# Summing, scaling and splitting the next chunk's x at set units of the first MoE's work

## The chip, the cores and the metric

The kernel runs on one core of one Trainium2 chip. The core has TensorE (matmuls, in profiles PE, its weight loads PEld), VectorE (DVE), ScalarE (ACT), GpSimd (POOL) and SyncE (SP), which here only issues DMAs. Each takes its own queue in order; they wait for one another by semaphores. The metric is the device time of one execution in microseconds (us); the median of several runs counts.

## The reference

Attention with a block mask over 4 batches x 8 heads (576 tokens of 64), then a gated MLP over all 2304 tokens ("moe1"), then a top-2 MoE with 8 experts. Cut to what matters:

```python
scores = np.where(mask, q @ k.T / 8, -1e9)               # per head, mask of 64x64 blocks
attn = np.exp(scores - scores.max(-1))
x = attn / (attn.sum(-1) + 1e-9) @ v                     # 2304 x 512, heads side by side
h = (x @ w1) * (x @ w2) @ w3                             # moe1
x = h @ w_out
logits = x @ w_gate + log1p(exp(x @ w_noise)) * noise    # router, top 2 of 8 experts
for e in range(8):                                       # moe2
    out[mask_e] += weight * (relu(x[mask_e] @ m1[e]) @ m2[e])
```

All matmuls run in fp32r with operands split into a high part and the rest (three matmuls for one product, `mm3`, L462 to L464).

## The kernel before

Attention goes head by head (32 heads). For each head `prep_h` splits q and k (hi on ScalarE and VectorE, L580 to L583; kl on GpSimd, L585), `s_unit` computes scores (L612, L615), `s_max` their maxima (nm, VectorE L626) and exponentials (pb, ScalarE L631), `g_unit` transposes (tp, L645) and splits the result (pt, ScalarE L649, VectorE L651), `av_a`/`av_b` multiply by v (L658, L670). The unnormalised output of a head goes to DRAM in two halves (x2, L674 on SP); after the last head of a batch the reciprocal sums go there too (rs, L685).

moe1 works on 9 chunks of 256 tokens. For chunk c, `x_load` (L147) reads both halves of x2 into xab (L160) and the reciprocal sums, spread over partitions, into xr (L165), all by SP. `x_prep` (L178) has three steps: the sum of the halves on GpSimd (L183), the scaling on VectorE (L186), and the split into xh (ScalarE L453, VectorE L457). The tiles xab, xr and xh have one buffer each, so the loads of a chunk wait until the scaling and the split of the one before have read their tiles. Then come eight units `ab` (L192): 24 matmuls on xh and the weights pc, a copy on ScalarE (at, L203), a product on VectorE (L204), and a split into gt (ScalarE L453, GpSimd L457). I write unit 3.4 for f = 4 of chunk 3. After the eight units `yout` (L208) multiplies gt by w3 @ w_out, in four blocks, and a `router` of small VectorE steps runs beside the next chunk. During the first units the weights are still converted from 64-bit words (stg, stf, L520 to L522 on VectorE) and split (pc).

`steps` (L361) is a generator that writes all this down; the attention loop draws from it ("f" in the table `LATER`), so heads and moe1 are interleaved, and what is left when the heads end is drawn alone. `ahead(c + 1, step)` writes the next chunk's load and its three preparation steps among the units of chunk c. Chunks 2, 4 and 6 need a batch whose heads end while the chunk before runs; theirs are written when `self.ready` allows. The order in each engine's queue is not the written one: a scheduler sorts the instructions by priority and by its own estimate of time, and `ab` and `yout` are written at a lower priority (`MOE_PRIO`) than the rest, `x_prep` among it.

Of the kernel before, what the change touches and what calls it, by code (L numbers as in the profile page):

```python
# [14 lines left out]
OP = mybir.AluOpType  # L15
# [14 lines left out]
CH = 256  # L30
NCH = NT // CH
# [31 lines left out]
ZC, NF = 3, 10  # L63
PIECE_PRIO, W_PRIO, MOE_PRIO = -60, -400, -200

FIRST = "g0 g1 t f1.3 c t o g2 g3 t p s0 t t s1 s2 f1.3 c t a f1.3 t b0 t s3 h t t c c b1 v l"
# [7 lines left out]
def r32(ap):  # L76
    return ap.bitcast(F32)


class Moe1:  # L80


    def __init__(self, k, p2, psM):
        self.k, self.tc, self.nc, self.a, self.p2 = k, k.tc, k.nc, k.a, p2
        self.psM = self.psR = psM
        self.p2s = ExitStack()
        self.ready, self.rt, self.ticks, self.conv = 0, iter(()), 1, 0
        self.xs, self.gts, self.ys, self.lg = {}, {}, {}, {}
        self.scat = []

    def setup_load(self):
        nc, a, p2 = self.nc, self.a, self.p2
# [99 lines left out]
    def ab(self, c, f):  # L192
        nc, p2, x = self.nc, self.p2, self.xs[c]
        ps = self.psM.tile([P, 512], F32, name="m")
        fo = (f % 2) * P
        for i, n in enumerate(("w1", "w2")):
            w = self.wp[n, f // 2]
            for dt in range(4):
                o = dt * 256 + fo
                self.k.mm3(ps[:, i * CH:(i + 1) * CH], (w[:, 0, o:o + P], w[:, 1, o:o + P]),  # L200
                           (x.h[:, 0, dt, :], x.h[:, 1, dt, :]), dt == 0, dt == 3)
        at = self.p2b.tile([P, CH], F32, name="at", bufs=2)
        nc.scalar.copy(at, ps[:, 0:CH])  # L203
        nc.vector.tensor_tensor(at, at, ps[:, CH:], op=OP.mult)  # L204
        gt = self.gts[c, f] = self.p2b.tile([P, 2, CH], F32R, name="gt", bufs=8)
        self.k.split((gt[:, 0, :], gt[:, 1, :]), at, low="pool")

    def yout(self, c, t, part):  # L208
        nc, p2 = self.nc, self.p2
# [150 lines left out]

    def steps(self):  # L361

        state = {}

        def ahead(c, step):

            if c == NCH or state.get(c, 0) != step or (step == 0 and self.batches(c) > self.ready):
                return
            if step == 0:
                self.x_load(c)  # L370
            else:
                self.x_prep(c, step - 1)
            state[c] = step + 1

        for c in range(NCH):
            for step in range(4):
                while state.get(c, 0) == step:
                    ahead(c, step)
                    yield 0
            for f in range(8):  # L380
                while self.conv < 28 + 4 * (f // 2):
                    yield 0
                with self.tc.high_priority(offset=MOE_PRIO):
                    self.ab(c, f)
                self.tick(self.ticks)
                if c == NCH - 1 and f % 2 == 1:
                    self.k.load_next()
                    self.k.load_next()
                if f in (0, 1, 2):
                    ahead(c + 1, 0)  # L390
                elif f == 4:
                    ahead(c + 1, 1)
                elif f == 6:
                    ahead(c + 1, 2)
                yield 2.67
            ahead(c + 1, 3)
            if c == NCH - 1:
                for _ in self.rt:
                    pass
                self.freeze()  # L400
            for t in range(TPC):
                for part in range(2):
                    with self.tc.high_priority(offset=MOE_PRIO):
                        self.yout(c, t, part)
                    self.tick(self.ticks)
                    yield 2.6
            for _ in self.rt:
                pass
            self.rt = self.router(c)
# [33 lines left out]
class Kernel:  # L443
# [5 lines left out]
    def split(self, dst, src, act="act", low="dve"):  # L449
        nc = self.nc  # L450
        h, l = dst
        if act == "act":
            nc.scalar.copy(h, src)  # L453
        else:
            nc.vector.tensor_copy(h, src)
        eng = nc.vector if low == "dve" else nc.gpsimd
        eng.tensor_tensor(l, src, r32(h), op=OP.subtract)  # L457

    def mm3(self, out, lh, rh, first, last):
        nc = self.nc  # L460
# [576 lines left out]
```

## Time and profile before

| | |
|---|---|
| three runs | 1132.89, 1132.94, 1134.70 us (median 1132.94) |
| the profiled execution | 1133.57 us, of which the span of the core is 1131.8 us |
| mean granted TensorE clock | 0.97 of full speed |
| TensorE busy | 1064.8 us, 94% of the span |
| VectorE, ScalarE, GpSimd busy | 576.9, 495.2, 371.4 us |
| attention and moe1 together | about 140 to 510 us |
| moe1 alone, then moe2 | about 510 to 640 us, then to the end |

A timeline row gives the start, the time it took, the engine, the line and the tiles; in brackets how long the engine had been idle and what ended that. A window row gives busy time in a stretch for each engine, then TensorE's granted clock (1.00 is 2.4 GHz, 0.50 is 1.2 GHz), then DMA. The chain of waits follows the end of the program back to what it hung on. Idle time matters where the engine is the one that the others have to wait for.

### The profile page before, as it was taken

The page shows a single profiled execution, that of the slowest core. Times are in us where ns is not written, and L with a number is a line of the kernel's source. Part 1 is how long each engine was busy: PE and PEld are TensorE (multiplying, and loading weights), DVE is VectorE, ACT ScalarE, POOL GpSimd, SP SyncE. Part 2 cuts the span into 40 slices and gives each one's busy share as a digit, 9 for nine tenths or more (in the row PEclk, how much of TensorE's full clock was granted, in tenths as well). Part 3 has the DMA queues.
Part 4 walks back from the last instruction along what each step waited for, and adds up shares of the span by engine and source line. Part 5 has one row for each costly group of instructions (what it writes and reads, how often), then busy time and mean ns, then how long its engine had stood idle before and what let it go on. Part 6 is the DMA issues. An engine that isn't in the chain of part 4 may idle for free.

```text
span 1131.8 us, 17580 instructions
## 1 busy us (share of the span) xinstructions
PE 1064.8 (94%) x6588; PEld 950.7 (84%) x6588; DVE 576.9 (51%) x1229; ACT 495.2 (44%) x1180; POOL 371.4 (33%) x355
## 2 busy tenths in 40 slices
PE   5899978999899989999999998999999999999996
PEld 3677767899798979998898797989899998989894
DVE  5897779667475847644443533543334342424110
ACT  5765546565466646642233314433333333333120
POOL 4443455525232442414422316332222222120202
PEclk9899988999899999999999999999999999999998
DMA  9765775325432484416213318745454545341203
GB/s 230 235 190 174 186 182 182 98 90 146 135 104 74 147 180 122 88 41 142 42 38 59 121 26 254 208 122 121 122 121 122 121 117 127 102 113 30 38 10 40
DMA packets 79443, 135.82 MB, mean 120 GB/s; under 512 B 21005, under 2 KB 45813, under 8 KB 79349
## 3 DMA queue, kind: packets, MB, share of 16 engines
q1 hardware_dynamic: 69237, 113.44, 35.4%
q0 software_dynamic: 10112, 21.16, 10.0%
q8 instruction: 54, 0.88, 0.3%
q14 instruction: 40, 0.33, 0.1%
HBM read 103.92 MB, written 30.66 MB: 119 GB/s over the span
## 4 chain that ended last, share of the span: by engine, by line
PE 72%; DMA 11%; DVE 10%; issue 3%; ACT 2%; POOL 2%; SPq 1%; POOLq 0%; DVEq 0%; ACTq 0%
PE ph L462 12%; PE ph L464 12%; PE ph L463 12%; PE m L462 7%; PE m L464 7%; PE m L463 7%; PE tp L645 3%; PE av L670 3%; DMA xr<-rs 2%; PE sb L615 2%; PE sb L612 2%; DMA stg<-in_w_dram 2%; PE m L885 2%; DVE stf L521 1%; DVE hi L582 1%
## 5 line engine op out<-in xcount | busy, mean ns | idle before, releaser
L462 PE MATMUL m<-xh,pc 128*128 128x256 f32 x576 | 166.4, 293 | 4.4 <-DVE at L204 2.0
L463 PE MATMUL m<-xh,pc 128*128 128x256 f32 x576 | 163.8, 288 | 2.6 <-DVE xh L457 2.6
L464 PE MATMUL m<-xh,pc 128*128 128x256 f32 x576 | 162.0, 287 | 4.0 <-POOL pc L457 4.0
L462 PE MATMUL ph<-xt,pc 128*128 128x256 f32 (+1 forms) x512 | 157.0, 308 | 4.6 <-ACT xt L453 4.6
L463 PE MATMUL ph<-xt,pc 128*128 128x256 f32 (+1 forms) x512 | 157.4, 308 | 0.0
L464 PE MATMUL ph<-xt,pc 128*128 128x256 f32 (+1 forms) x512 | 157.1, 307 | 0.0
L898 DVE SCALAR_TENSOR_TENSOR ht<-ph,ht 128x256 fp32r<-128x256 f32 (+1 forms) x128 | 61.8, 489 | 131.5 <-ACT ht L897 128.4
L912 POOL DMA_INDIRECT out_dram<-yo,ids x40 | 64.7, 1617 | 195.4 <-ACT yo L911 102.6
L462 PE MATMUL ph<-pc,ht 128*128 128x512 f32 x320 | 128.0, 401 | 0.0
L463 PE MATMUL ph<-pc,ht 128*128 128x512 f32 x320 | 126.3, 395 | 0.0
L464 PE MATMUL ph<-pc,ht 128*128 128x512 f32 x320 | 126.2, 395 | 0.0
L631 ACT ACTIVATE pb<-sb,nm 128x288 f32<-128x288 f32 (+3 forms) x192 | 93.6, 497 | 73.8 <-DVE nm L629 38.8
L457 DVE TENSOR_TENSOR pc<-stf,pc 128x1024 fp32r<-128x1024 f32 x56 | 67.4, 1225 | 102.2 <-ACT pc L453 98.7
L453 ACT CAST pc<-stf 128x1024 fp32r<-128x1024 f32 (+1 forms) x96 | 82.1, 872 | 81.2 <-DMA stf<-in_m_dram 47.9
L462 PEld LDWEIGHTS m<-xh,pc 128*128 128x128 f32 x576 | 110.6, 193 | 6.9 <-DVE at L204 2.9
L464 PEld LDWEIGHTS m<-xh,pc 128*128 128x128 f32 x576 | 110.0, 194 | 4.7 <-POOL pc L457 4.4
L463 PEld LDWEIGHTS m<-xh,pc 128*128 128x128 f32 x576 | 110.5, 193 | 4.0 <-DVE xh L457 3.3
L897 ACT ACTIVATE ht<-ph 128x256 fp32r<-128x256 f32 (+1 forms) x128 | 55.2, 437 | 130.9 <-PE ph L464 129.2
L457 POOL TENSOR_TENSOR gt<-at,gt 128x256 fp32r<-128x256 f32 x72 | 60.4, 841 | 140.2 <-ACT gt L453 137.7
L462 PEld LDWEIGHTS ph<-xt,pc 128*128 128x128 f32 x512 | 96.6, 189 | 5.2 <-ACT xt L453 4.9
L463 PEld LDWEIGHTS ph<-xt,pc 128*128 128x128 f32 x512 | 96.6, 189 | 0.3
L464 PEld LDWEIGHTS ph<-xt,pc 128*128 128x128 f32 x512 | 96.6, 189 | 0.0
(157 smaller groups left out, 2298.8 us busy)
## 6 DMA issues: line engine op xcount, KB each, us to landing
stf<-in_m_dram SPq DMA_DIRECT2D x56, 512.0 KB
qk<-in_qk_dram SPq DMA_DIRECT2D x32, 576.0 KB
stg<-in_w_dram SPq DMA_DIRECT2D x32, 512.0 KB
x<-ev SPq DMA_DIRECT2D x32, 288.0 KB
xab<-x SPq DMA_DIRECT2D x20, 256.0 KB
yt<-y SPq DMA_DIRECT2D x18, 260.0 KB
stg<-in_w_out_dram SPq DMA_DIRECT2D x8, 512.0 KB
v<-in_v_dram SPq DMA_DIRECT2D x24, 160.0 KB
```

The source lines that it names most:

```text
L453: nc.scalar.copy(h, src)
L457: eng.tensor_tensor(l, src, r32(h), op=OP.subtract)
L462: nc.tensor.matmul(out, a, c, start=first, stop=False)
L463: nc.tensor.matmul(out, a, d, start=False, stop=False)
L464: nc.tensor.matmul(out, b, c, start=False, stop=last)
L612: nc.tensor.matmul(o, lh, c.hi[:, 1, k0:k0 + w], start=True, stop=False)
L631: nc.scalar.activation(pb[t][:, k0:k0 + src.free_size()], src, AF.Exp, bias=nm, scale=1.0, accum_out=sums[:, h // H, t + n, h % H:h % H + 1])
L645: nc.tensor.transpose(bank[:, n * P:(n + 1) * P], pb[t][:, kt * P:(kt + 1) * P], self.ident)
L670: nc.tensor.matmul(c.av[:, o0:o0 + w], c.vv[:, kt, :], c.pt[:, i, s0:s0 + w], start=(kt == 0 and i == 0), stop=(kt == 4 and i == m - 1))
L897: nc.scalar.activation(hh[:, 0, f, :], ph, AF.Relu)
L898: nc.vector.scalar_tensor_tensor(hh[:, 1, f, :], ph, 0.0, r32(hh[:, 0, f, :]), op0=OP.max, op1=OP.subtract)
L912: nc.gpsimd.indirect_dma_start(out=self.a["out"], out_offset=self.idx(e, i), in_=yo, in_offset=None, compute_op=OP.add)
```

## The change

The scheme of calls is replaced by a clock. `clock` counts the units, each f and each block of `yout`; after a step is written, `due` forbids the next one for `AHEAD[step]` = 4, 2, 1, 0 counts (for chunk 0 none). With the load written at unit c.0, the sum is written after unit c.4, the scaling after c.6 and the split after c.7, as before; but the priority no longer sets their place alone: each step of `x_prep` is written inside `issue_after` of the last unit's `marks`, which are its product on VectorE, its gt cast on ScalarE and its gt subtraction on GpSimd. So each engine's part of a step stands in that engine's queue behind its part of that unit. A step that is late because its batch wasn't ready can now also fall between the blocks of `yout`. `split` returns its two instructions for this.

```diff
@@ -63,6 +63,8 @@
 ZC, NF = 3, 10
 PIECE_PRIO, W_PRIO, MOE_PRIO = -60, -400, -200
 
+AHEAD = [4, 2, 1, 0]
+
 
 
 FIRST = "g0 g1 t f1.3 c t o g2 g3 t p s0 t t s1 s2 f1.3 c t a f1.3 t b0 t s3 h t t c c b1 v l"
@@ -86,7 +88,7 @@
         self.p2s = ExitStack()
         self.ready, self.rt, self.ticks, self.conv = 0, iter(()), 1, 0
         self.xs, self.gts, self.ys, self.lg = {}, {}, {}, {}
-        self.scat = []
+        self.scat, self.marks = [], ()
 
     def setup_load(self):
         nc, a, p2 = self.nc, self.a, self.p2
@@ -201,9 +203,9 @@
                            (x.h[:, 0, dt, :], x.h[:, 1, dt, :]), dt == 0, dt == 3)
         at = self.p2b.tile([P, CH], F32, name="at", bufs=2)
         nc.scalar.copy(at, ps[:, 0:CH])
-        nc.vector.tensor_tensor(at, at, ps[:, CH:], op=OP.mult)
+        v = nc.vector.tensor_tensor(at, at, ps[:, CH:], op=OP.mult)
         gt = self.gts[c, f] = self.p2b.tile([P, 2, CH], F32R, name="gt", bufs=8)
-        self.k.split((gt[:, 0, :], gt[:, 1, :]), at, low="pool")
+        self.marks = (*self.k.split((gt[:, 0, :], gt[:, 1, :]), at, low="pool"), v)
 
     def yout(self, c, t, part):
         nc, p2 = self.nc, self.p2
@@ -360,23 +362,31 @@
 
     def steps(self):
 
-        state = {}
-
-        def ahead(c, step):
-
-            if c == NCH or state.get(c, 0) != step or (step == 0 and self.batches(c) > self.ready):
+        state, due = {}, {}
+        clock = [0]
+
+        def ahead(c, last=3):
+
+
+
+            step = state.get(c, 0)
+            if c == NCH or step > last or clock[0] < due.get(c, 0) or (step == 0 and self.batches(c) > self.ready):
                 return
             if step == 0:
                 self.x_load(c)
             else:
-                self.x_prep(c, step - 1)
+                with ExitStack() as es:
+                    for m in self.marks:
+                        es.enter_context(self.tc.issue_after(m.ins))
+                    self.x_prep(c, step - 1)
             state[c] = step + 1
+            due[c] = clock[0] + (0 if c == 0 else AHEAD[step])
 
         for c in range(NCH):
-            for step in range(4):
-                while state.get(c, 0) == step:
-                    ahead(c, step)
-                    yield 0
+            while state.get(c, 0) < 4:
+                ahead(c)
+                clock[0] += 2
+                yield 0
             for f in range(8):
                 while self.conv < 28 + 4 * (f // 2):
                     yield 0
@@ -386,14 +396,10 @@
                 if c == NCH - 1 and f % 2 == 1:
                     self.k.load_next()
                     self.k.load_next()
-                if f in (0, 1, 2):
-                    ahead(c + 1, 0)
-                elif f == 4:
-                    ahead(c + 1, 1)
-                elif f == 6:
-                    ahead(c + 1, 2)
+                ahead(c + 1, 2)
+                clock[0] += 1
                 yield 2.67
-            ahead(c + 1, 3)
+            ahead(c + 1)
             if c == NCH - 1:
                 for _ in self.rt:
                     pass
@@ -403,6 +409,8 @@
                     with self.tc.high_priority(offset=MOE_PRIO):
                         self.yout(c, t, part)
                     self.tick(self.ticks)
+                    ahead(c + 1)
+                    clock[0] += 1
                     yield 2.6
             for _ in self.rt:
                 pass
@@ -450,11 +458,11 @@
         nc = self.nc
         h, l = dst
         if act == "act":
-            nc.scalar.copy(h, src)
+            d = nc.scalar.copy(h, src)
         else:
-            nc.vector.tensor_copy(h, src)
+            d = nc.vector.tensor_copy(h, src)
         eng = nc.vector if low == "dve" else nc.gpsimd
-        eng.tensor_tensor(l, src, r32(h), op=OP.subtract)
+        return d, eng.tensor_tensor(l, src, r32(h), op=OP.subtract)
 
     def mm3(self, out, lh, rh, first, last):
         nc = self.nc
```

How the queues change is shown at three places. The first is GpSimd, at the start of moe1, with chunk 1's sum: gt is the split of units 0.0 and 0.1, pc_ are weights, kl and vv belong to a head. Before:

```order
L457 TENSOR_TENSOR pc_71<-stf,pc_71 128x512
L457 TENSOR_TENSOR gt<-at,gt 128x256
L457 TENSOR_TENSOR pc_71<-stf,pc_71 128x512
L183 TENSOR_TENSOR xab<-xab 128x4x256
L457 TENSOR_TENSOR gt<-at,gt 128x256
L457 TENSOR_TENSOR pc_72<-stf,pc_72 128x512
L585 TENSOR_TENSOR kl<-qk,hi 128x576
```

After (lines are 2 higher up to the router, 8 higher from `split` on), the same stretch:

```order
L465 TENSOR_TENSOR pc_71<-stf,pc_71 128x512
L465 TENSOR_TENSOR gt<-at,gt 128x256
L465 TENSOR_TENSOR pc_71<-stf,pc_71 128x512
L465 TENSOR_TENSOR gt<-at,gt 128x256
L465 TENSOR_TENSOR pc_72<-stf,pc_72 128x512
L593 TENSOR_TENSOR kl<-qk,hi 128x576
```

And further down in the same queue of after, where the sum now stands:

```order
L593 TENSOR_TENSOR kl<-qk,hi 128x576
L601 TENSOR_TENSOR vv<-v,vv 128x5x64
L465 TENSOR_TENSOR gt<-at,gt 128x256
L185 TENSOR_TENSOR xab<-xab 128x4x256
L465 TENSOR_TENSOR gt<-at,gt 128x256
```

The sum of chunk 1 has left its place between the splits of units 0.0 and 0.1 and stands behind the gt of unit 0.4.

The second place is GpSimd with chunk 3's sum. Before, directly behind the gt of units 1.6 and 1.7:

```order
L593 TENSOR_TENSOR vv<-v,vv 128x5x64
L457 TENSOR_TENSOR gt<-at,gt 128x256 x2
L183 TENSOR_TENSOR xab<-xab 128x4x256
L585 TENSOR_TENSOR kl<-qk,hi 128x576
L593 TENSOR_TENSOR vv<-v,vv 128x5x64
L457 TENSOR_TENSOR gt<-at,gt 128x256
```

After, the same sum, behind the gt of unit 2.4:

```order
L465 TENSOR_TENSOR gt<-at,gt 128x256 x2
L593 TENSOR_TENSOR kl<-qk,hi 128x576
L465 TENSOR_TENSOR gt<-at,gt 128x256
L601 TENSOR_TENSOR vv<-v,vv 128x5x64
L465 TENSOR_TENSOR gt<-at,gt 128x256 x2
L185 TENSOR_TENSOR xab<-xab 128x4x256
L593 TENSOR_TENSOR kl<-qk,hi 128x576
```

The sum moved by five units; in between stand the head's kl and vv and the gt of units 2.0 to 2.4.

The third place is VectorE with chunk 3's scaling (xr), nm and pt being a head's maxima and transposes. Before, at the end of chunk 1's units:

```order
L204 TENSOR_TENSOR at<-at,m 128x256
L651 TENSOR_TENSOR pt<-tp,pt 128x448 x2
L626 TENSOR_REDUCE nm_2861<-sb 128x1
L626 TENSOR_REDUCE nm_2863<-sb 128x1
L626 TENSOR_REDUCE nm_2871<-sb 128x1
L626 TENSOR_REDUCE nm_2878<-sb 128x1
L186 TENSOR_TENSOR xr<-xab,xr 128x1024
L651 TENSOR_TENSOR pt<-tp,pt 128x512
```

After, behind the product (at) of unit 2.6, with the split's xh behind the product of 2.7:

```order
L333 CAST si<-sl 128x4
L354 TENSOR_TENSOR y<-oh_3732,oh_3792 128x8 x2
L206 TENSOR_TENSOR at<-at,m 128x256
L188 TENSOR_TENSOR xr<-xab,xr 128x1024
L634 TENSOR_REDUCE nm_3669<-sb 128x1
L634 TENSOR_REDUCE nm_3671<-sb 128x1
L659 TENSOR_TENSOR pt<-tp,pt 128x448
L634 TENSOR_REDUCE nm_3679<-sb 128x1
L659 TENSOR_TENSOR pt<-tp,pt 128x448
L634 TENSOR_REDUCE nm_3686<-sb 128x1
L206 TENSOR_TENSOR at<-at,m 128x256
L465 TENSOR_TENSOR xh<-xr,xh 128x1024
```

The scaling has left its place ahead of a head's pt and stands seven units later.

## Rows read from the trace of the kernel before

**Rows 1.** Windows of the whole core: us, then each engine's busy us, TensorE clock, DMA.

```profile
core 0: us, PE busy (x) PEld busy (x) DVE busy (x) ACT busy (x) POOL busy (x), PEclk, DMA share, GB/s
150.00:214.00 64.00, 55.22 (x359) 50.14 (x359) 54.70 (x94) 39.26 (x106) 37.20 (x27) 0.85 0.60 173
214.00:510.00 296.00, 285.79 (x2044) 263.48 (x2044) 183.49 (x474) 167.19 (x484) 97.94 (x94) 0.98 0.42 112
```

**Rows 2.** Chain of waits in order of time: start us, us, engine and tile.

```profile
276.89 10.45 DMA xab<-x
287.47 2.34 POOL xab L183
289.83 2.40 DVE xr L186
...
408.48 11.10 DMA xr<-rs
```

**Rows 3.** Timeline around chunk 3's sum: start, us, engine, operation, [idle <-releaser].

```profile
287.46 2.34 POOL L183 TENSOR_TENSOR xab<-xab 128x1024 f32<-128x1024 f32 x1 [8.28 <-DMA xr<-rs]
...
289.83 2.40 DVE L186 TENSOR_TENSOR xr<-xab,xr 128x1024 f32<-128x1024 f32 x1 [9.44 <-POOL xab L183]
...
292.89 0.69 PE L658 MATMUL tp<-pt,vv 128*128 128x128 f32 x2 [5.63 <-DVE pt L651]
```

**Rows 4.** The same view around chunk 5's sum.

```profile
412.50 2.34 POOL L183 TENSOR_TENSOR xab<-xab 128x1024 f32<-128x1024 f32 x1 [6.28 <-DMA xab<-x]
...
415.58 0.80 PE L464 MATMUL m<-pc,gt 128*128 128x512 f32 x1 [2.92 <-POOL gt L457]
```

**Rows 5.** The same view around chunk 1's sum, and one more hi row later.

```profile
162.37 2.36 POOL L183 TENSOR_TENSOR xab<-xab 128x1024 f32<-128x1024 f32 x1 [4.33 <-DMA xab<-x]
...
165.31 1.38 DVE L186 TENSOR_TENSOR xr<-xab,xr 128x1024 f32<-128x1024 f32 x1
...
167.86 0.58 PE L464 MATMUL m<-xh,pc 128*128 128x256 f32 x1 [3.63 <-POOL pc L457]
...
168.38 1.86 DVE L582 SCALAR_TENSOR_TENSOR hi<-qk,hi 64x576 fp32r<-64x576 f32 x1
...
269.34 0.76 DVE L582 SCALAR_TENSOR_TENSOR hi<-qk,hi 64x576 fp32r<-64x576 f32 x1
```

**Rows 6.** Windows behind those three idle times, columns as in the first group.

```profile
164.00:168.00 4.00, 0.37 (x4) 0.14 (x1) 3.72 (x5) 0.84 (x2) 4.00 (x4) 0.80 0.25 91
168.00:177.00 9.00, 9.00 (x39) 7.99 (x40) 8.70 (x14) 3.54 (x9) 5.33 (x4) 0.52 0.74 220
...
293.00:299.00 6.00, 6.00 (x27) 5.81 (x28) 2.16 (x6) 2.44 (x7) 0.87 (x1) 0.50 0.72 213
...
415.60:419.00 3.40, 3.40 (x8) 2.72 (x9) 0.00 (x0) 0.59 (x1) 2.12 (x2) 0.50 0.86 223
```

**Rows 7.** SP's queue: waits in 404 to 426 us (us, times, longest), then its timeline.

```profile
SPq L160 <- DVE nm L626: 9.0, 1, 9.0
...
311.58 0.38 SPq L674 DMA_DIRECT2D x<-ev  x1
324.61 0.38 SPq L674 DMA_DIRECT2D x<-ev  x1
```

**Rows 8.** Timeline from chunk 8's split to its first matmul.

```profile
595.40 1.41 DVE L457 TENSOR_TENSOR xh<-xr,xh 128x1024 fp32r<-128x1024 f32 x1 [3.06 <-issue]
...
606.31 0.36 PE L462 MATMUL m<-xh,pc 128*128 128x256 f32 x1
```

**Rows 9.** Timeline around chunk 8's sum; last row: all of L271, ns min/median/max.

```profile
539.91 2.37 POOL L183 TENSOR_TENSOR xab<-xab 128x1024 f32<-128x1024 f32 x1 [10.66 <-DMA xab<-x]
...
540.88 1.44 DVE L271 TENSOR_SCALAR u<-ez 128x16 f32<-128x16 f32 x1 [0.28 <-ACT ez L268]
...
544.88 0.40 PE L462 MATMUL m<-xh,pc 128*128 128x256 f32 x1 [1.49 <-DVE at L204]
...
L271 DVE TENSOR_SCALAR u<-ez x9: 164/174/1439, 251.1 to 653.9; 128x16 f32<-128x16 f32 x9
```

## The prediction

> **What bounds the kernel now.** I first read the windows of the whole core. From 214 to 510 us TensorE is busy 285.79 of 296.00 us at clock 0.98, while VectorE has 183.49 and GpSimd 97.94 [rows 1]: in this stretch attention heads and moe1's units share TensorE, and its work is the bound. What a change can win there is TensorE's idle time and its half-clock time, and nothing else. From 150 to 214 us it is another case: TensorE 55.22 of 64.00, VectorE 54.70, clock 0.85 [rows 1]. There VectorE, which also converts the weights, is nearly full, and its queue sets the pace of the heads.
>
> Second, the chain of waits. In the saturated stretch it runs over TensorE's matmuls, but near 277 us it leaves them: a load of x (10.45 us), its sum on GpSimd, its scaling on VectorE, and only then other work [rows 2]. Near 408 us it goes over a load of the reciprocal sums, 11.10 us [rows 2]. Third, the timeline at these places. At chunk 3 GpSimd sits 8.28 us before the sum, VectorE 9.44 us before the scaling (2.40 us), and TensorE 5.63 us for a pt tile of an attention head [rows 3]. That tile has nothing to do with x; its subtraction merely stands behind the scaling in VectorE's queue. At chunk 5 GpSimd sits 6.28 us before the sum, the gt tile of a moe1 unit is queued behind it, and TensorE waits 2.92 us for that gt [rows 4]. At chunk 1 the sum starts after 4.33 us of idle GpSimd, a pc tile of the weights is queued behind it, and TensorE waits 3.63 us for that [rows 5]. So three of the nine boundaries have one fault: the steps of the next x stand in the queues before their data has landed, and unrelated work stands behind them. After each of these idle times TensorE's granted clock is at 1.2 GHz for a while: 0.50 in 293 to 299 and in 415.6 to 419, 0.52 in 168 to 177 [rows 6].
>
> **Part by part.** The arithmetic stays: ten sums of x on GpSimd, ten scalings, ten splits, and the same loads. Only their places move. In the order of the changed kernel the sum of chunk c+1 stands behind the gt of unit c.4, the scaling behind the product of unit c.6, the split behind unit c.7, for every chunk from 1 on; before, the sums for chunks 1, 3, 5, 7 and 8 stood at units 0.0, 1.7, 3.6, 5.7 and 5.7, directly behind their loads. An edge joins two instructions of one engine, which takes its queue in order anyway, so it adds no instruction and no wait between engines; I price the edges at 0.
>
> Chunk 3: its sum moves from behind unit 1.7 to behind unit 2.4, five units and a second stage later, so the load that was 8.28 us late has landed. What goes is 5.63 us of idle TensorE [rows 3] and the half clock after it: 6.00 us of full work at 0.50 would have been 3.00 us at 2.4 GHz [rows 6]. Sum 5.63 + 3.00 = 8.6 us. All of it lies on the path, since TensorE is what bounds this stretch. If the cover fails the upper price is zero gain; I see no reason for it, as the head's own pt, which is next, waited for nothing but its place in the queue.
>
> Chunk 5: the sum moves from behind unit 3.6 to behind 4.4. What goes is 2.92 us idle [rows 4] and 3.40 us at 0.50, that is 1.70 us [rows 6]. Sum 4.6 us, same argument. SP gains too: its load of x for chunk 6 waited 9.0 us for a VectorE queue that was itself held by the scaling [rows 7], with the store of a head's output and the next q and k behind it.
>
> Chunk 1 is harder to price. TensorE loses 3.63 us here [rows 5] and then 9.00 us at clock 0.52, which is 4.3 us more [rows 6]; that would be 7.9 us if TensorE were the bound. But VectorE is busy 3.72 of 4.00 and 8.70 of 9.00 us of the same windows [rows 6], so the head would be late anyway. The lower end is the scaling's own 1.38 us [rows 5], which leaves this full queue for unit 0.6, where the conversions are over. Between the ends: the hi of the next head took 1.86 us beside a GpSimd that was working off its backlog, against 0.76 us for another [rows 5], 1.10 us more. I take 1.38 + 1.10 = 2.5 us, since VectorE's busy share is the row nearest to this place, and keep 1.4 and 7.9 for the range.
>
> Chunks 2, 4 and 6 need heads that end late; their sums stay at units 1.4, 3.4 (from 3.3) and 5.4 (from 5.3), so nothing is booked. Chunks 7 and 8 cause no idle TensorE at their loads, so moving them wins nothing there.
>
> What gets later is the split: in the old queues ScalarE's half stood before the copy of unit c.7, now it stands behind it and behind the gt of c.7. It could not start sooner in either case than the last matmul that reads the old xh. For chunk 8 the split ended at 596.8 and its first matmul was at 606.31 [rows 8]: 9.5 us, filled by the four second-stage blocks of the chunk before. It now stands behind one more copy, product and cast of 128x256, each a quarter of the split's own size (1.41 us on VectorE [rows 8]); even at 0.5 us each, an estimate from that row, it ends 1.5 to 2 us later, so over 7 us of cover are left, and I price this at 0. If that cover were gone, each microsecond would count once per chunk. The loads move too: those for the next chunk wait for the scaling (unit c.6) and the split (c.7), and behind them on SP stand the store of one head, and q, k and v of another. A head takes 13 us here: outputs of two heads are stored at 311.58 and 324.61 [rows 7]. These loads are one head ahead, so I price it at 0 as well and keep a rival for it.
>
> Last, the sum now always runs beside a unit's work. At chunk 8 it ran from 539.91 for 2.37 us, VectorE's tiny L271 beside it took 1.44 us against a median of 0.174, and TensorE then waited 1.49 us [rows 9]. In the pure moe1 stretch two sums now stand at such places, units 6.4 and 7.4, where one did: from -1.5 to +1.5 us, I take 0.
>
> The Trainium skill (SBUF — State Buffer, SBUF: two separate sides) says that VectorE and GpSimd lock a shared port pair for whole instructions, so that one of them fully blocks. The trace agrees: 1.44 us for an instruction of 0.17 beside the sum [rows 9]. By that rule alone every sum in the middle of a unit would be a cost, which speaks against the change; it is the rival D below.
>
> **Sum.** 8.6 + 4.6 + 2.5 = 15.7 us off the profiled execution's 1133.57 us gives 1117.9 us. That execution is 0.6 us above the median of the three runs (1132.94), so I expect 1117 us.
>
> **Rivals.** A: the wait moves on. The head at the boundary finds the next obstacle (the exponentials on ScalarE, or kl on GpSimd), and half of the 15.7 us stays: about 1126 us. For it: a new order reshuffles every queue from unit 0.6 on. Against: outside these three places TensorE idles little in 296 us.
> B, on the slow side: SP's queue. The loads for the next x now block SP until the split, and the q and k of a head stand behind them. If SP is held longer than a head lasts (13 us), hi is late and TensorE idles as it did at chunk 3: 8.6 us each. From two such places on the gain of 15.7 us is gone, and five (chunks 1 to 5) give 1133 - 15.7 + 43 = 1160 us; three give 1143. Against: the longest such wait before was 9.0 us [rows 7], and it held no head up by itself.
> C: the change does not do what it says, because the scheduler had put the steps there already or the stalls are caused by something else: 1133 us. The order speaks against it.
> D: sums beside a unit cost 1.49 us each [rows 9] wherever they stand. Eight sums (chunks 1 to 8), one of them paid already: 7 x 1.49 = 10.4 us back, 1128 us. Against: in the mixed stretch GpSimd's sums for chunks 2 and 4 already stood inside units and TensorE was busy 285.79 of 296.00 us.
>
> **How the numbers follow.** Forecast 0.66; A 0.17; D 0.08; B 0.06; C 0.03. The range goes down to 1109: chunk 1 at 7.9 instead of 2.5 (1112), the 1.49 us of chunk 8 gone (1110), and a little for other half-clock time before 214 us. It goes up to 1128: all of A, and D at its price. Left out is B, C and the tails, less than 0.2. A measurement of this kernel can tell about 0.2% (2.3 us) from no change. Faster: the forecast, nearly all of A and D, 0.89. Within 0.2%: C and bits of A and D, 0.05. Slower: B, 0.06.
>
> **What would show it.** Right: no idle time of TensorE near chunk 3's and chunk 5's starts; GpSimd's sum with no wait for a load at chunks 1, 3, 5, 7; the windows after them at clock 1.00. Chunk 1's term: VectorE still full from 150 to 214 us, and the stretch 1.4 to 8 us shorter. Wrong: SP waits over 10 us with a late hi behind them (B); TensorE waiting for at or gt after each sum (D); TensorE idle for xh at a chunk's first matmul, which would mean that the cover of 7 us was not there.

## The result, and the profile after

The changed kernel takes 1124.47 us (median of eight runs), against 1135.68 us for the kernel before. The ratio of all runs of the two is 0.991, 95% interval 0.9886 to 0.9934. That is faster by 0.9%, or 10.2 us on the profiled execution's 1133.57 us (the medians lie 11.2 us apart); the forecast was 15.7. The profiled execution of after took 1124.48 us, its span 1122.7 us, at a mean granted clock of 0.979 instead of 0.97. The experiments below ran on four chips, on which the kernel before takes about 1141 to 1143 us, so I give each as a ratio to the kernel before on the same chip.

The windows of after, with the columns of [rows 1]; the third and fourth windows are two half-clock stretches that this kernel has:

```profile
150.00:214.00 64.00, 50.31 (x342) 45.01 (x341) 53.03 (x91) 37.65 (x101) 32.96 (x26) 0.92 0.59 167
214.00:510.00 296.00, 290.60 (x2109) 269.06 (x2109) 187.81 (x494) 171.74 (x494) 102.97 (x99) 0.99 0.44 115
205.00:208.20 3.20, 3.15 (x13) 2.94 (x14) 1.13 (x2) 2.64 (x10) 0.85 (x1) 0.52 0.00 0
269.80:276.20 6.40, 5.72 (x27) 5.28 (x28) 3.96 (x19) 3.03 (x9) 2.79 (x3) 0.50 0.51 132
```

Read TensorE's busy time times the clock, roughly the work done. From 214 to 510 us it was 285.79 x 0.98 = 280.1 before and is 290.60 x 0.99 = 287.7: 7.6 us more. The clock is printed to two digits, so each of these long products is good to 1.5 us. From 150 to 214 us it was 55.22 x 0.85 = 46.9 and is 50.31 x 0.92 = 46.3: nothing gained. Here VectorE is as full as before (53.03 of 64).

That "nothing" is a gain and a loss. The same stretch cut at 190 us, two rows of before and then two of after; chunk 1's sum stood in the first part (at 162 us) and now stands in the second (at 198 us):

```profile
150.00:190.00 40.00, 33.64 (x207) 30.55 (x207) 33.52 (x57) 21.80 (x58) 21.97 (x16) 0.80 0.71 193
190.00:214.00 24.00, 21.58 (x154) 19.59 (x153) 21.18 (x38) 17.46 (x49) 15.23 (x11) 0.92 0.42 139
150.00:190.00 40.00, 33.77 (x228) 30.20 (x228) 31.87 (x59) 23.16 (x62) 18.94 (x16) 0.91 0.77 207
190.00:214.00 24.00, 16.54 (x116) 14.81 (x114) 21.16 (x33) 14.49 (x40) 14.03 (x10) 0.93 0.30 101
```

Around the old place TensorE's work rose from 26.9 to 30.7 us, all of it by the clock, since its busy time is the same. Around the new place it fell from 19.9 to 15.4 us.

GpSimd's waits for x are gone. The view of one line (the row of its instructions, then the idle time of GpSimd ahead of them), before and then after:

```profile
L183 POOL TENSOR_TENSOR xab<-xab x10: 729/2368/2394, 134.5 to 539.9; 128x1024 f32<-128x1024 f32 x8, 128x768 f32<-128x768 f32 x1, 128x256 f32<-128x256 f32 x1
its engine sat idle before it (us, times) until:
  DMA xab<-x: 34.7, 7
  DMA xr<-rs: 8.3, 1
```

```profile
L185 POOL TENSOR_TENSOR xab<-xab x10: 911/2392/2817, 134.3 to 578.6; 128x1024 f32<-128x1024 f32 x8, 128x768 f32<-128x768 f32 x1, 128x256 f32<-128x256 f32 x1
its engine sat idle before it (us, times) until:
  DMA xab<-x: 6.4, 1
```

The one wait left is chunk 0's, which has nothing to hide behind. The sums of chunks 3 and 5 in after's timeline, with what answers to [rows 3] and [rows 4]: no bracket behind either sum, so GpSimd was busy up to it. But look at hi in the second group.

```profile
328.66 2.40 POOL L185 TENSOR_TENSOR xab<-xab 128x1024 f32<-128x1024 f32 x1
...
450.67 2.38 POOL L185 TENSOR_TENSOR xab<-xab 128x1024 f32<-128x1024 f32 x1
450.83 2.83 DVE L590 SCALAR_TENSOR_TENSOR hi<-qk,hi 64x576 fp32r<-64x576 f32 x1
...
453.81 0.33 PE L620 MATMUL sb<-hi 128*128 128x192 f32 x1 [1.47 <-DVE hi L590]
```

An instruction of VectorE that takes 0.76 us elsewhere [rows 5] took 2.83 us beside the sum, and TensorE waited 1.47 us for it. The same happened at the sum of chunk 1, at unit 0.4, which answers to [rows 5]:

```profile
197.94 2.82 POOL L185 TENSOR_TENSOR xab<-xab 128x1024 f32<-128x1024 f32 x1
...
198.44 2.60 DVE L528 TENSOR_SCALAR stf<-stg 128x512 int32<-128x512 int32 x1
...
205.05 1.09 PE L653 MATMUL tp<-ident,pb 128*128 128x128 f32 x4 [4.86 <-DVE pt L659]
...
208.71 0.42 DVE L528 TENSOR_SCALAR stf<-stg 128x512 int32<-128x512 int32 x1
```

The conversion L528 took 2.60 us beside the sum and 0.42 us ten microseconds later. VectorE's queue is full here, so the head's pt slipped behind it, TensorE idled 4.86 us, and its clock fell to 0.52 (the third window above). The hold itself is 2.2 us of this; the rest is what stood in the queue ahead of pt. And at chunk 2's sum:

```profile
265.86 2.39 POOL L185 TENSOR_TENSOR xab<-xab 128x1024 f32<-128x1024 f32 x1
...
266.04 2.24 DVE L313 CAST mb<-mk 128x16 bf16<-128x16 f32 x1
...
268.22 1.40 POOL L593 TENSOR_TENSOR kl<-qk,hi 128x576 fp32r<-128x576 f32 x1
268.28 1.35 DVE L348 TENSOR_TENSOR e<-e,w 128x2 f32<-128x2 f32 x1
268.34 0.17 PE L321 MATMUL m<-mb,tri 128*128 128x16 bf16 x1 [0.67 <-DVE mb L313]
...
269.89 0.90 PE L653 MATMUL tp<-ident,pb 128*128 128x128 f32 x3 [1.38 <-DVE ev L668]
...
271.40 0.50 PE L620 MATMUL sb<-hi 128*128 128x192 f32 x1 [0.59 <-DVE hi L590]
```

A router cast of 16 columns took 2.24 us, the next small step 1.35 us beside kl, and TensorE lost 0.67 + 1.38 + 0.59 = 2.64 us and then 5.72 us of work at clock 0.50, another 2.9 us. So the old idle times at chunks 3 and 5 left and new ones came: TensorE is full from 284 to 300 and, but for 0.1 us, from 400 to 430 us, at clock 1.00 both times. The experiments are to tell which part of the change did what.

Two terms priced at nothing can be read here too. The split of chunk 8, [rows 8] of before, with the first matmul that needs it:

```profile
587.40 1.45 DVE L465 TENSOR_TENSOR xh<-xr,xh 128x1024 fp32r<-128x1024 f32 x1 [1.42 <-ACT xh L461]
...
596.44 0.36 PE L470 MATMUL m<-xh,pc 128*128 128x256 f32 x1
```

It ends at 588.85, 7.6 us ahead: the cover of over 7 us held. On SP, by the view of its waits from 150 to 510 us, no load of x waited over 3.3 us, where 9.0 us stood in [rows 7]. Its longest wait of any kind grew, from 11.6 to 13.7 us; it is a head's store that waits for its own data, and TensorE's waits for hi in the mixed stretch (2.1 us in all) are those of the holds shown above.

### The profile page after: what moved, and what is told of

It reads as the page before. It is cut to its first block, busy times and chain, and to the rows that moved or that the text cites. A ratio compares the mean times of both kernels' runs of the same rounds, so it can differ in the third digit from the quotient of the medians.

```text
span 1122.7 us, 17570 instructions
## 1 busy us (share of the span) xinstructions
PE 1056.7 (94%) x6588; PEld 945.3 (84%) x6588; DVE 575.1 (51%) x1229; ACT 496.8 (44%) x1180; POOL 367.5 (33%) x355
## 3 DMA queue, kind: packets, MB, share of 16 engines
q0 software_dynamic: 10112, 21.16, 10.2%
## 4 chain that ended last, share of the span: by engine, by line
PE 72%; DMA 10%; DVE 9%; issue 3%; ACT 2%; POOL 2%; SPq 2%; POOLq 0%; DVEq 0%; ACTq 0%
PE ph L470 12%; PE ph L472 12%; PE ph L471 12%; PE m L470 7%; PE m L471 7%; PE m L472 7%; PE tp L653 3%; PE av L678 3%; DMA stg<-in_w_dram 3%; DMA v<-in_v_dram 2%; PE sb L623 2%; PE sb L620 2%; DMA out_dram<-yo,ids 2%; DVE stf L529 2%; PE m L893 1%
## 5 line engine op out<-in xcount | busy, mean ns | idle before, releaser
L465 POOL TENSOR_TENSOR gt<-at,gt 128x256 fp32r<-128x256 f32 x72 | 57.8, 807 | 156.3 <-ACT gt L461 153.5
L653 PE MATMUL tp<-ident,pb 128*128 128x128 f32 x480 | 83.0, 289 | 23.3 <-ACT pb L639 8.4
L470 PEld LDWEIGHTS ph<-xt,pc 128*128 128x128 f32 x512 | 96.5, 189 | 5.6 <-issue 4.0
L634 DVE TENSOR_REDUCE nm<-sb 128x1 f32<-128x128 f32 (+2 forms) x192 | 79.2, 438 | 38.2 <-PE sb L623 32.9
```

The source lines that it names most:

```text
L465: return d, eng.tensor_tensor(l, src, r32(h), op=OP.subtract)
L470: nc.tensor.matmul(out, a, c, start=first, stop=False)
L634: nc.vector.tensor_reduce(nm[:, n:n + 1], o[:, 0:w], axis=AX, op=OP.max, negate=True)
L653: nc.tensor.transpose(bank[:, n * P:(n + 1) * P], pb[t][:, kt * P:(kt + 1) * P], self.ident)
```

## The experiments

Theory at the start: the edges act and the terms for chunks 3 and 5 are right, and a part of the gain was lost to the sums that now run beside VectorE's work (the rival D of the prediction). Rival: the clock of calls did the work, and what is missing was never there.

### Edges and clock apart

The first run leaves out the edges and keeps the clock; the second keeps the call scheme of before and has the edges alone.

```diff
-                with ExitStack() as es:
-                    for m in self.marks:
-                        es.enter_context(self.tc.issue_after(m.ins))
-                    self.x_prep(c, step - 1)
+                self.x_prep(c, step - 1)
```

> The changed kernel with its clock (4, 2, 1 units apart) kept, but the order edges left out: the three steps of x_prep are written plainly, and priority and the scheduler's estimate set their place. Theory: the edges act, not the clock; without them the steps drift ahead to directly behind their loads, the idle times of TensorE at chunks 3 and 5 (5.63 and 2.92 us) and the half clock behind them come back, and the ratio to the kernel before is 0.998 to 1.003. Rival: the clock alone places the steps, and the ratio stays at 0.991, as with edges.

Measured: 1.000 (0.9981 to 1.0019). Without the edges the two idle times are back at chunks 3 and 5, 6.85 and 4.68 us in this run (timeline of the kernel without edges):

```profile
287.56 2.34 POOL L185 TENSOR_TENSOR xab<-xab 128x1024 f32<-128x1024 f32 x1 [9.42 <-DMA xab<-x]
...
292.98 0.69 PE L663 MATMUL tp<-pt,vv 128*128 128x128 f32 x2 [6.85 <-DVE pt L656]
...
413.74 2.34 POOL L185 TENSOR_TENSOR xab<-xab 128x1024 f32<-128x1024 f32 x1 [7.97 <-DMA xab<-x]
...
416.81 0.79 PE L469 MATMUL m<-pc,gt 128*128 128x512 f32 x1 [4.68 <-POOL gt L462]
```

> The kernel before with its own scheme of calls (sum written at unit 4, scaling at unit 6, split after unit 7), and nothing added but the order edges to the last unit's product, cast and subtraction. Theory: the edges alone carry the change; no GpSimd wait for a load of x at chunks 1, 3, 5 and 7, ratio to the kernel before 0.989 to 0.993. Rival: the clock matters too, for chunks whose batch is late (2, 4, 6), and then the ratio lies between 0.993 and 1.000.

Measured: 0.9897 (0.9864 to 0.9931), the same as the changed kernel. GpSimd waits for no load of x from chunk 1 on in this run either. So the edges carry the change and the clock adds nothing that can be measured.

### Chunks 3 and 5, and chunk 1, by themselves

```diff
-                    for m in self.marks:
+                    for m in (self.marks if c in (3, 5) else ()):
```

> The changed kernel with the order edges for chunks 3 and 5 alone: their sums stand at units 2.4 and 4.4, those of chunks 1, 2, 4, 6, 7 and 8 where the kernel before has them (units 0.0, 1.4, 3.3, 5.3, 5.7, 5.7). Theory: the two terms of 8.6 and 4.6 us are right, and what the change lost elsewhere (4.86 us of idle TensorE and half clock behind the sum of chunk 1 at its new place) is absent: ratio 0.986 to 0.990. Rival: the two terms were over-sized and part of the gain belongs to the other chunks: 0.991 to 0.996.

Measured: 0.9882 (0.9861 to 0.9903), or 13.5 us of 1140.73 (interval 11.1 to 15.9); the two terms were 8.6 + 4.6 = 13.2. The windows say how (columns as above). Windows of two traces differ a little by themselves: from 214 to 510 us the kernel without edges, as fast as before, has 282.97 x 0.98 = 277.3 us of work where before has 280.1, so I read nothing into differences under 3 us there.

```profile
214.00:510.00 296.00, 294.51 (x2138) 271.73 (x2138) 190.76 (x505) 172.28 (x496) 110.81 (x101) 1.00 0.47 118
510.00:640.00 130.00, 121.22 (x818) 110.20 (x817) 48.62 (x164) 38.90 (x85) 43.41 (x45) 0.97 0.32 71
```

In the mixed stretch TensorE is as good as full, 294.5 us of work against 280.1, more than the two terms asked for. In the pure stretch it lost some: GpSimd had idled 9.12 us before chunk 8's sum, still at its early place, and TensorE then stood 2.99 us, with its clock at 0.89 on average from 530 to 560 us.

```profile
530.19 2.36 POOL L185 TENSOR_TENSOR xab<-xab 128x1024 f32<-128x1024 f32 x1 [9.12 <-DVE ln L286]
...
534.15 0.58 PE L470 MATMUL m<-xh,pc 128*128 128x256 f32 x1 [2.99 <-DVE at L206]
```

So the total agrees with the sum of the two terms, though it is made of a larger gain and a loss. That the waits go is shown; the size of the two terms is borne out by the total alone.

With `c in (1,)` in the same line, chunk 1 is alone:

> The changed kernel with the order edges for chunk 1 alone: its sum stands at unit 0.4 instead of 0.0, the sums of the others within two units of where the kernel before has them, chunks 3 and 5 keeping their early places. Theory: at its new place the sum costs TensorE as much as at the old one (4.86 us idle instead of 3.63, less half clock), so the term of chunk 1 is near zero: ratio 0.998 to 1.002. Rival 1, the prediction: 2.5 us won, 0.997 to 0.998, and up to 7.9 us, 0.993. Rival 2: the new place is worse, above 1.002.

Measured: 1.0028 (1.0009 to 1.0047), slower by 3.2 us (interval 1.0 to 5.4). The value is Rival 2's (its interval reaches into the theory's range), and the prediction's +2.5 us did not hold. The timeline repeats what the changed kernel shows: a conversion L528 of 2.62 us beside the sum, and then 4.33 us of idle TensorE for a pt.

TensorE's work (busy time times clock) around the two places of chunk 1's sum, in the one traced execution of each kernel of this document, says more than the total:

| where chunk 1's sum stands | kernels | 150 to 190 us | 190 to 214 us |
|---|---|---|---|
| unit 0.0 | before; without edges; edges for chunks 3 and 5 | 26.9 to 28.9 | 18.5 to 19.9 |
| unit 0.4 | changed; edges only; edge for chunk 1; chunk 1 at c.4, the others at c.6 | 30.0 to 31.3 | 14.4 to 15.4 |
| behind unit 0.6 or 0.7 | the four runs of that kind below | 29.2 to 31.4 | 18.1 to 18.9 |
| unit 0.4, but on VectorE | below | 30.6 | 20.1 |
| left out | below | 30.8 | 20.5 |
| unit 0.4, in quarters | below | 27.3 | 19.3 |

Leaving unit 0.0 brings TensorE some 3 us in the first part, wherever the sum goes (the quarters are the one exception, and I don't know why). A whole GpSimd sum at unit 0.4 costs some 4 us in the second, and no other place or form of it does. The two make up only a part of the 3.2 us; in this run the sums of chunks 2 to 5 also stood up to two units from their old places, and how much of the loss is theirs isn't settled.

13.5 - 3.2 = 10.3 us is what the whole change brought, but that is partly luck: the edges for chunks 3 and 5 alone lose at chunk 8, which the changed kernel doesn't, and the changed kernel loses at the sums of chunks 2 and 5 (2.64 + 2.9 and 1.47 us above), which that one doesn't.

### What the sums cost, and on which engine

The next run leaves the addition out: the halves are loaded, but the scaling reads the first half alone.

> The changed kernel without the sum: the two halves of x are loaded as before, but nothing adds them, and the scaling reads the first half alone. The sum's part of the computation is left out. It bounds what all ten sums cost where they now stand. Theory: the sums at chunks 1 and 2 cost some 6 us each with the half clock behind them, the others little, ratio 0.979 to 0.986. Rival: other instructions become late in their place and the waits of TensorE at these places stay, ratio 0.989 to 0.993.

Measured: 0.9767 (0.9732 to 0.9801), below the theory's range: the ten sums of 2.8 us and less, none of them on TensorE, cost the changed kernel about 1.4%.

```diff
-                nc.gpsimd.tensor_tensor(x.ab[:, g:e, 0, :], ...
+                nc.vector.tensor_tensor(x.ab[:, g:e, 0, :], ...
```

> The changed kernel with the sum of the two halves of x on VectorE instead of GpSimd, at the same units, behind the product instead of the gt subtraction. Theory: what the change gave back is the pairing of a 2.4 us GpSimd sum with small VectorE instructions (L528 took 2.60 instead of 0.42 us beside chunk 1's sum, L313 2.24 instead of 0.16 us beside chunk 2's); with the sum on VectorE these two places lose their waits of TensorE (4.86 us, and 0.67 + 1.38 + 0.59 us) and the half clock behind them, ratio 0.982 to 0.988. Rival 1: it is VectorE's queue that is short of time at these two places, and a sum in that queue holds it as long as one beside it: ratio 0.989 to 0.993, as the changed kernel. Rival 2: the sum takes longer than 2.4 us of VectorE's queue per chunk and delays the heads: above 0.993.

Measured: 0.9901 (0.9872 to 0.993), Rival 1's figure. The theory was half right: with the sum on VectorE (1.22 us each) the 4.86 us behind chunk 1's sum are gone (the longest wait of TensorE from 192 to 212 us is 1.3 us), which speaks, with the table above, for the hold as their cause, but other waits came elsewhere. TensorE's waits for hi from 214 to 510 us (us, times, longest) were 2.1, 2, 1.5 in the changed kernel and are

```profile
PE sb L620 <- DVE hi L590: 5.5, 4, 2.0
```

```diff
-                nc.gpsimd.tensor_tensor(x.ab[:, g:e, 0, :], ...
+                for i in range(g, e):
+                    nc.gpsimd.tensor_tensor(x.ab[:, i, 0, :], ...
```

> The changed kernel with each sum of 128x1024 written as four of 128x256 on GpSimd, at the same place. Theory: a VectorE instruction beside a sum waits for the end of the one GpSimd instruction that it met, so it loses at most a quarter (some 0.7 us instead of 2.2); the idle times of TensorE behind the sums of chunks 1 and 2 shrink and the half clock behind them goes: ratio 0.983 to 0.989, with VectorE rows of under 1.2 us beside the quarters. Rival: VectorE is held until all four are through, or held four times, and the ratio stays at 0.990 or above.

Measured: 0.9879 (0.9857 to 0.9902), at the upper end of the theory's range; its interval overlaps that of the changed kernel, so a gain over it isn't shown. No VectorE row is held for a whole sum any more, but several in turn are held for a part of one (the first row holds all four quarters):

```profile
266.84 3.33 POOL L186 TENSOR_TENSOR xab<-xab 128x256 f32<-128x256 f32 x4
...
267.59 0.70 DVE L318 TENSOR_TENSOR run<-run,mk 128x8 f32<-128x8 f32 x1
...
268.39 1.18 DVE L591 SCALAR_TENSOR_TENSOR hi<-qk,hi 64x576 fp32r<-64x576 f32 x1
```

Cutting the sum up spreads the hold; what it brings, 0.3% by these two ratios, is within the noise.

### Another place for the sum

```diff
-AHEAD = [4, 2, 1, 0]
+AHEAD = [6, 0, 1, 0]
```

> The changed kernel with the sum two units later, at units c.6 (scaling and split both behind c.7), for every chunk. Theory: what a sum costs hangs on which VectorE instructions happen to run beside it, so another place moves the cost, with a sum over eight places within 5 us of the changed kernel: ratio 0.987 to 0.995. Rival 1: the place at c.4 in the stretch where VectorE is full was the fault, and at c.6, when the conversions are over, the cost goes: below 0.987. Rival 2: the cover of 7 us for the split is eaten and TensorE waits for xh at each chunk's first matmul: above 0.995.

Measured: 0.9769 (0.9748 to 0.979). Rival 1's range, and as fast as without any sum. The theory, that another place only moves the cost about, fell. Rival 1's reason, the full VectorE queue, can explain chunk 1 alone; the gain here lies behind that stretch too. From 214 to 510 us TensorE is full, and the view of its waits in this stretch has one line (us, times, longest):

```profile
214.00:510.00 296.00, 295.65 (x2140) 272.55 (x2138) 189.16 (x501) 170.28 (x487) 107.41 (x102) 1.00 0.45 117
```

```profile
PE sb L620 <- ACT pb L639: 0.3, 1, 0.3
```

Chunk 2's sum shows what stands beside it there:

```profile
275.14 2.39 POOL L185 TENSOR_TENSOR xab<-xab 128x1024 f32<-128x1024 f32 x1
275.99 0.69 DVE L659 TENSOR_TENSOR pt<-tp,pt 128x512 fp32r<-128x512 f32 x1 [1.47 <-ACT pt L657]
```

At unit c.6 the router of the chunk before is mostly through: of the eight sums only chunk 6's holds a router step (a cast, 2.03 us). Beside the sum VectorE has only a pt, which reads tp from PSUM and takes its usual 0.69 us, and then waits for the sum itself. Chunk 1's sum begins at 213.82 us, and the last conversion L528 had started at 204.3.

Two runs share the gain out: chunk 1 alone at c.6 with the others at c.4, and the reverse.

```diff
+AHEAD_1 = [6, 0, 1, 0]
-            due[c] = clock[0] + (0 if c == 0 else AHEAD[step])
+            due[c] = clock[0] + (0 if c == 0 else (AHEAD_1 if c == 1 else AHEAD)[step])
```

> The changed kernel with the sum of chunk 1 alone two units later (unit 0.6, its scaling and split behind 0.7); all other sums stay behind units c.4. The kernel with all sums at c.6 had a ratio of 0.977, the changed kernel 0.991; this run and its counterpart share the 1.4% out. Theory: both parts count, since a sum holds up VectorE wherever small instructions stand beside it: chunk 1 is worth about 0.005 (the 0.0028 that its edge alone cost, and the 2.5 us of the prediction, now won), ratio 0.984 to 0.988. Rival 1: all of it is chunk 1's place in the full VectorE queue: 0.975 to 0.980. Rival 2: nothing of it: 0.989 to 0.993.

Measured: 0.9833 (0.9809 to 0.9857).

> The counterpart: the sum of chunk 1 stays behind unit 0.4, the sums of chunks 2 to 8 stand behind units c.6. Theory: seven sums at places without small VectorE instructions beside them win some 9 us, chunk 1 keeps its loss: ratio 0.980 to 0.984. Rival 1 (all is chunk 1's): 0.989 to 0.993. Rival 2 (nothing is chunk 1's): 0.975 to 0.979.

Measured: 0.9825 (0.98 to 0.985). Both parts count, as the theory had it (the first a little more than it allowed): 0.991 - 0.9833 = 0.0077 for chunk 1, 0.991 - 0.9825 = 0.0085 for the seven others, together 0.016 where the joint step gave 0.014. Each difference is good to some 0.003, and they are not clean shares: with chunk 1 alone at c.6, chunk 2's loss of above went too, though its sum stayed at unit 1.4. These two kernels also show that a hold need not cost much. With chunk 1 at c.6, the sum of chunk 2 still stood at unit 1.4 and held a router step for 2.05 us:

```profile
263.28 2.41 POOL L186 TENSOR_TENSOR xab<-xab 128x1024 f32<-128x1024 f32 x1 [1.51 <-DMA xab<-x]
263.66 2.05 DVE L350 TENSOR_TENSOR oh<-oh,w 128x16 f32<-128x16 f32 x1
```

and TensorE waited 0.4 us in all from 262 to 272 us. In the reverse kernel a hi came up beside the end of a gt and was held through three more GpSimd instructions in a row, and TensorE waited 0.95 us:

```profile
337.94 5.75 DVE L591 SCALAR_TENSOR_TENSOR hi<-qk,hi 64x576 fp32r<-64x576 f32 x1
...
338.48 2.40 POOL L186 TENSOR_TENSOR xab<-xab 128x1024 f32<-128x1024 f32 x1
340.83 1.42 POOL L594 TENSOR_TENSOR kl<-qk,hi 128x576 fp32r<-128x576 f32 x1
342.22 0.85 POOL L602 TENSOR_TENSOR vv<-v,vv 128x320 fp32r<-128x320 f32 x1
...
343.75 0.35 PE L621 MATMUL sb<-hi 128*128 128x192 f32 x1 [0.95 <-DVE hi L591]
```

### All steps behind c.7, and a hold put there on purpose

```diff
-AHEAD = [4, 2, 1, 0]
+AHEAD = [7, 0, 0, 0]
```

> The changed kernel with sum, scaling and split all behind unit c.7 (7, 0, 0 units). In the pure moe1 stretch a unit takes 2.9 us and with the sum at c.6 the split ended about 3.5 us ahead of the next chunk's first matmul, so about 0.6 us of the cover is left. Theory: the cover just holds or lacks 1 us at chunks 7 and 8 alone: ratio 0.976 to 0.980, TensorE waiting for xh at most 2 us in all. Rival: the cover is gone at most chunks, TensorE waits for xh 1 us or more at five or more of them with half clock behind: above 0.982.

Measured: 0.976 (0.974 to 0.9779). At chunk 8 the split ends at 585.2 and the first matmul is at 587.84, so 2.6 us of the cover are left (I had reckoned with 0.6), and TensorE waits for xh at chunk 0 alone.

To this kernel the last run adds a copy of 16 columns on VectorE, ready just as the sum begins:

```diff
+            if c > 0:
+                sm = self.p2.tile([P, 16], F32, name="sm")
+                lo = self.gts[c - 1, 7][:, 1, 0:16]
+                nc.vector.tensor_copy(sm, lo.bitcast(F32))
```

> The kernel with all three steps behind unit c.7 (ratio 0.976), with one suspected cost added for each of chunks 1 to 8: a copy of 128x16 on VectorE that reads 16 columns of the gt subtraction which stands ahead of the sum on GpSimd, so that it comes up as the sum begins; its output is not used. Alone such a copy takes some 0.2 us. Theory: beside the sum it takes about 2.2 us wherever it falls into it, which shows the hold by itself; but at this place TensorE has the next unit's and the second stage's matmuls queued (no idle over 0.6 us from 214 to 510 us in the kernel without the copy), so the holds cost little: ratio 0.975 to 0.980. Rival: a held VectorE costs TensorE its time wherever it is, as it did beside the sums of chunks 1 and 2 at c.4: 0.982 to 0.990. Third: the copy isn't held (under 0.5 us), and then the long rows of before and after have another cause.

Measured: 0.9739 (0.9714 to 0.9764), no slower than without the copy, so the theory held. The view of its line (ns, min/median/max) and the window of the mixed stretch:

```profile
L189 DVE COPY sm<-gt x8: 1682/2354/2361, 217.9 to 579.2; 128x16 f32<-128x16 f32 x8
```

```profile
214.00:510.00 296.00, 295.36 (x2143) 272.80 (x2143) 202.33 (x511) 170.67 (x491) 109.95 (x104) 1.00 0.44 118
```

VectorE was held at all eight sums, 2.35 us at most of them, and is busy 12.4 us longer from 214 to 510 us (202.33 against 189.97 without the copy); TensorE is full all the same. So the hold is there at each of these sums, and at this place it costs no time. That its price hangs on what TensorE has queued at the place is my reading; the runs show that TensorE stayed full, not why.

## Why the prediction was right or wrong

Direction and range held: faster, and 1124 lies in 1109 to 1128. The size did not: 15.7 us were forecast, 10.2 came.

**Chunks 3 and 5** (8.6 + 4.6 us): the mechanism is shown. The loads land ahead of the sums, the idle times of [rows 3] and [rows 4] are gone with the half clock behind them, and without the edges they are back. The edges for these two chunks alone give 13.5 us in total, with a loss at chunk 8 inside it, so the size fits but isn't measured term by term.

**Chunk 1** (+2.5 us, bounds 1.4 to 7.9): this is the step that failed. For the old place the term was about right: leaving it brings some 3 us (the table above; 3.8 us between before and after). But the prediction priced only what leaves the full VectorE queue for unit 0.6, the scaling, and put the sum's new place, unit 0.4, at nothing, with no row for it. At 198 us that place is still inside the stretch that the prediction itself had called full; the sum held a conversion there for 2.60 us, and TensorE lost some 4 us (4.5 us between before and after). So the stretch gained nothing, and the edge alone made the kernel slower, outside the term's bounds. Two units later the sum costs TensorE nothing that can be read there.

**Sums beside units** (-1.5 to +1.5 us, taken as 0, for the pure stretch; for chunks 2 and 4 "nothing is booked"): right for chunk 8, whose wait of 1.49 us [rows 9] went. Not right in the mixed stretch, where the sums of chunks 2 and 5 cost 2.64 + 2.9 and 1.47 us. The argument was that sums had already stood inside units there while TensorE was busy. They were not free: before, chunk 4's sum held a router step for 2.27 us and TensorE waited 0.91 us for the cast behind it, as it waits 0.91 us in after:

```profile
389.67 2.27 DVE L306 TENSOR_TENSOR mk<-oh,oh 128x16 f32<-128x16 f32 x1
...
392.68 0.17 PE L319 MATMUL m<-mb,tri 128*128 128x16 bf16 x1 [0.91 <-DVE mb L311]
```

Chunk 2's sum held a router cast too, and TensorE then waited for nothing that came behind it. I take that for luck: a change which shifts the heads against the units deals anew what stands beside a sum. Why the hold at chunk 2 is dear in one order and free in another I have not shown; in the dear one a second hold, beside kl, follows at once, but so it does in one of the free ones.

**Rival D**, given 0.08, had the mechanism, with a price that was too even: 1.49 us at each sum. A hold by the sum was there at seven of the eight sums (VectorE rows of 1.04 to 2.83 us; at chunk 3 only a pt stood beside it) and cost from nothing to 6.4 us (4.86 us and 3.15 us of work at clock 0.52). The time, 1124, lies nearer to D and A (1128 and 1126) than to the forecast (1117); the range held because D and A had been taken into it.

The Trainium skill (SBUF — State Buffer, Who interferes with whom) says that a VectorE instruction with two SBUF inputs, or in a two-port mode, contends with GpSimd's reads and the later of the two fully blocks, and that one with at most one SBUF input outside these modes does not. The traces agree: hi and run, with two inputs in SBUF, were held (2.83 and 2.28 us), and pt, which reads PSUM, kept its 0.68 us beside a sum. The casts were held too (2.24 us); in which mode they ran no trace shows.

**Edges at 0, the later split at 0, SP at 0**: nothing speaks against them. The edges' kernel shows no wait that I could put down to an edge, the split's cover was 7.6 us, and loads of x wait less on SP. Rival C did not happen, nor B: SP's longest wait is over 13 us now, but no hi is late by it. A did not happen at chunks 3 and 5; at chunk 1 something like it did: from 150 to 190 us TensorE is busy as long as before, with waits for ev and pt of up to 2.10 us in place of the 3.63 us.

The largest miss is not in the sum at all: the place c.4, which change and prediction took as given, leaves some 1.4% behind. With all three steps behind c.7, or the sum at c.6, the kernel is 2.3 to 2.4% faster than before, ahead of both kernels.

## What to carry to other kernels

When a step is moved out of a queue where it waited for its data, price it at its new place as carefully as at the old one: what runs on the other engines beside it there, and who waits for that. In this kernel the long GpSimd sum did best where VectorE had only PSUM readers beside it or where TensorE stayed full; which engine does it, or in how many pieces, mattered less than where it stands. Where a scheduler sorts by its own estimate, an order edge on the same engine's queue was enough to hold a step in place, at no cost that I could measure.

## What the runs showed of the hardware that I had not expected

A copy of 16 columns on VectorE took 2.35 us beside a GpSimd sum of 2.40 us, at seven of eight places: held to the sum's end, where a cast of this size takes 0.17 us elsewhere. A hold can run over several GpSimd instructions: 5.75 us through the end of a gt, a sum, a kl and a vv, where the instruction takes 0.76 us alone. The same sum of 128x1024 takes 2.39 us on GpSimd and 1.22 us on VectorE. And TensorE's idle time can stay while the time falls: from 150 to 510 us TensorE was busy 341.0 us before and 340.9 us after, and what changed was the granted clock, 0.85 to 0.92 up to 214 us and 0.98 to 0.99 behind it.
